# Block 0 of a two-layer transformer kernel: the fourth tile's transposition given to a DMA, and two Q chunks begun for three tiles

## The chip, the cores and the metric

The kernel runs on one core of a Trainium2 chip. The metric is the device time of one execution in microseconds (us), taken as the median of repeated runs.

## The reference

The input `x` has 2048 tokens of 1024 features in bf16. A layer normalisation, an attention and a residual sum are followed by a layer normalisation, a gated feed-forward part and a residual sum; the pair is done twice with the same weights.

```python
qkv = layernorm(x) @ wqkv                      # 32 heads of 32
idx = pos[:, None] - (arange(8) * 2)[None, :]  # 8 keys, every second token back
attn = softmax(q . k[idx] * 32**-0.5)          # negative positions masked
x = x + (attn @ v[idx]) @ wo
h = relu(layernorm(x) @ W_gate) * (layernorm(x) @ W_up)   # 3584 wide
x = x + h @ W_down
```

## The kernel before

The 2048 tokens are four blocks of 512, and a block is four tiles of 128 tokens. All of `x` stays in SBUF as sixteen tiles `x0` to `x15`. Matmuls need the normalised block with features on partitions, `xnT`, an array of tile, feature chunk (eight of 128) and token.

Only block 0 of the first layer is touched by the change. Its layer normalisation is `ln_first` and its V product is `v_first`; they are written out by hand, tile by tile, so that TensorE can start while most of the data is still in flight. The steps that matter:

- `bn` and `aggr` make mean and variance of a tile on VectorE, `power` makes the reciprocal deviation on GpSimd, and `apply(t)` writes the normalised tile into `xn_first` on VectorE.
- `turn(t)` transposes a tile with eight TensorE transposes into a PSUM tile (`tp_pair`); `copy(t, "v", 0)` and `copy(t, "a", 1)` bring the two halves into `xnT_first`, one on VectorE and one on ScalarE. `later(t)` is these three for tiles 2 and 3.
- Tile 0 is multiplied before its deviation is known. `scaled(i)` multiplies the deviation into its part of V; `widen` multiplies it into tile 0 of `xnT_first`, so that Q and K can use that tile as it is.
- `prod(kc, c, t0, t1)` is one V matmul: weight chunk `kc`, output chunk `c`, tiles `t0` to `t1`. Tiles 0 and 1 share the PSUM tiles `pairs[0, i]`, tiles 2 and 3 the PSUM tiles `pairs[1, i]`, one for each two output chunks. `halves(i, part, k0)` finishes one of these.

After V come sixteen groups `acc_q` and `acc_k` of eight matmuls with 512 columns (`qk_steps`), in the order q0, q1, q2, k0, q3, k1 and so on. ScalarE copies every finished PSUM tile to SBUF.

Weights are loaded in slabs of 1 MB into a ring of five buffers (`wring`): both halves of V (`v0, 0` for `kc` 0 to 3 and `v0, 1` for `kc` 4 to 7), both halves of Q, both of K. The sixth slab, the second half of K, takes the buffer of `v0, 0` and so can only be loaded when the last matmul that reads `v0, 0` is done. Nearly all DMAs are issued by SyncE (SP) in one written order (`sp_dma` ties each to the one before); in block 0 that order is the V slices with `x2` and `x3` among them, Q, `x4` and `x5`, the first K slab, the second K slab, `x6` to `x11`, and then the transposing DMAs of block 1 (`xnT_a`). ScalarE's queue issues only a part of `x0` and `x1`.

PSUM has six buffers for products, so a new product may have to wait until ScalarE or VectorE has read an old one. TensorE's order is fixed by `pe_group`, VectorE's by `dv`, ScalarE's in this part by `on("a", ...)`. Events with a planned time (`ev`) only set the order in which the program is written.

Of the kernel before, what the change touches and what calls it, by code (L numbers as in the profile page):

```python
# [8 lines left out]
F32 = mybir.dt.float32  # L9
# [4 lines left out]
P = 128  # L14
# [6 lines left out]
KC = D // P  # L21
BLK = 512
TPB = BLK // P
# [13 lines left out]
def kernel(  # L37
# [11 lines left out]
    nc = tc.nc  # L49
# [31 lines left out]
    psum = ctx.enter_context(tc.tile_pool(name="psum", bufs=6, space=bass.MemoryType.PSUM))  # L81
# [41 lines left out]
    @contextmanager  # L123
    def pe_group():
        if tail_pe[0] is None:
            yield
        else:
            with tc.issue_after(tail_pe[0]):
                yield

    def mm(*args, **kwargs):
        tail_pe[0] = nc.tensor.matmul(*args, **kwargs).ins  # L132
# [51 lines left out]
    slab = {}  # L184
# [9 lines left out]
    def qkv_half(i, hh):  # L194
        return wqkv_v[:, hh * (KC // 2):(hh + 1) * (KC // 2), i * D:(i + 1) * D]
# [26 lines left out]
    def load_slab(key, src):  # L222
        shp = list(src.shape)
        t = wring.tile([P, 8 * SLAB], BF16, tag="slab", name="w_" + "_".join(str(k) for k in key))
        tv = t[:, 0:shp[1] * shp[2]].rearrange("p (a b) -> p a b", b=shp[2])
        if key[0] == "v0":
            for i, (k0, k1) in enumerate(((0, 1), (1, 2), (2, 3), (3, 4)) if key[1] == 0 else ((0, 1), (1, 2), (2, 3), (3, 4))):
                if (key[1], i) == (1, 2):
                    load_x(0, [2, 3])
                sp_dma(tv[:, k0:k1, :], src[:, k0:k1, :])  # L230
        else:
            sp_dma(tv, src)
        slab[key] = tv
# [71 lines left out]
    load_slab(("v0", 0), qkv_half(2, 0))  # L305
    load_slab(("v0", 1), qkv_half(2, 1))
    load_slab(("qk01", "q", 0), qkv_half(0, 0))

    ones = const.tile([P, P], BF16, name="ones")
    nc.vector.memset(ones[:], 1.0)  # L310
# [9 lines left out]
    def ln_first():  # L320
# [94 lines left out]
        def open_up():  # L415
# [12 lines left out]
            apply(1, 0)  # L428
            apply(1, 1)

        hold.update(on=on, bn=bn, aggr=aggr, apply=apply, turn=turn, copy=copy, widen=widen,
                    spread_rstd=spread_rstd, open_up=open_up, last=last)
        return hold

# [3 lines left out]
    def v_steps(n, ln, key, early=False):  # L438
# [15 lines left out]

        return [f_(c) for c in range(KC)]

    def v_first(ln):
        st = att[0]
        pairs, opened = {}, set()

        def prod(kc, c, t0, t1):
            part = t0 // 2
            if (part, c // 2) not in pairs:
                pairs[part, c // 2] = psum.tile([P, 2, BLK // 2], F32, tag="acc", name="acc_v")
            acc = pairs[part, c // 2][:, c % 2, (t0 % 2) * P:(t0 % 2 + t1 - t0) * P]
            with pe_group():
                mm(acc, lhsT=slab["v0", kc // (KC // 2)][:, kc % (KC // 2), c * P:(c + 1) * P],
                   rhs=ln["xnT"][:, t0:t1, kc, :], start=(part, c // 2) not in opened, stop=(kc == KC - 1),
                   skip_group_check=True)
            opened.add((part, c // 2))  # L470

        def scaled(i):
            dv(nc.vector.tensor_tensor, st["vT"][:, 2 * i:2 * i + 2, 0:P], pairs[0, i][:, :, 0:P],
               _ap(ln["rb"], 0, [[0, 2], [1, P]]), op=ALU.mult)

        def later(t):
            ln["turn"](t)
            ln["copy"](t, "v", 0)
            ln["copy"](t, "a", 1)

        def halves(i, part, k0):
            for c in (2 * i, 2 * i + 1):
                for kc in range(k0, KC):
                    prod(kc, c, 2 * part, 2 * part + 2)

        def head():
            st["vT"] = big_tile([P, KC, BLK], "vT_0", True)
            ln["open_up"]()

            def chunk(kc, t):  # L490
                for c in range(KC):
                    prod(kc, c, t, t + 1)

            for kc in range(4):
                chunk(kc, 0)
            ln["turn"](1, (0,))
            ln["copy"](1, "v", 0)
            ln["turn"](1, (1,))
            ln["copy"](1, "a", 1)
            chunk(4, 0)  # L500
            for kc in range(5):
                chunk(kc, 1)
            ln["spread_rstd"]()
            chunk(5, 0)
            chunk(5, 1)
            ln["bn"](2, 0)
            ln["bn"](2, 1)
            ln["aggr"](2)
            ln["bn"](3, 0)
            ln["apply"](2)  # L510
            ln["bn"](3, 1)
            ln["aggr"](3)
            for i in range(KC // 2):
                if i == 2:
                    later(2)
                    scaled(1)
                    ln["apply"](3)
                halves(i, 0, 6)
                if i != 1:
                    scaled(i)  # L520
                ln["on"]("a", nc.scalar.copy, st["vT"][:, 2 * i:2 * i + 2, P:2 * P], pairs[0, i][:, :, P:2 * P])
            for t in (2, 3):
                for c in range(KC):
                    if (t, c) == (2, KC // 2):
                        later(3)
                        ln["widen"]()
                    for kc in range(KC // 2):
                        prod(kc, c, t, t + 1)
            for i in range(KC // 2):
                halves(i, 1, KC // 2)  # L530
                ln["on"]("a", nc.scalar.copy, st["vT"][:, 2 * i:2 * i + 2, 2 * P:BLK], pairs[1, i][:])
            tail_act[0] = ln["last"]["a"]

        return head
# [17 lines left out]
    def qk_steps(n, ln, key, staged=False):  # L552
        b = n % NB
        st = att[n]
        staging = {}

        def tile_of(nm, c, cols):
            if staged:
                staging[nm, c] = pool["stage"].tile([P, BLK], BF16, tag="st", name=f"{nm}st_{n}_{c}")
                return staging[nm, c][:]  # L560
            t = qk_pool.tile([P, cols], BF16, tag=nm, name=f"{nm}_{n}_{c}")
            st[(nm, c)] = t
            return t[:]

        def f_(nm, c):
            def f():
                if nm == "k" and c == 0 and not staged:
                    khalo[n] = qk_pool.tile([P, KC, HALO], BF16, tag="kh", name=f"kh_{n}", bufs=2)
                acc = psum.tile([P, BLK], F32, tag="acc", name=f"acc_{nm}")
                with pe_group():  # L570
                    for kc in range(KC):
                        w = slab[(key, nm, kc // (KC // 2))][:, kc % (KC // 2), bass.ds(c, P, KC)]
                        mm(acc[:], lhsT=w, rhs=ln["xnT"][:, :, kc, :], start=(kc == 0), stop=(kc == KC - 1))
                if nm == "q":
                    q = tile_of("q", c, BLK)
                    tail_act[0] = nc.scalar.copy(q, acc[:]).ins
                elif staged:
                    tail_act[0] = nc.scalar.copy(tile_of("k", c, BLK), acc[:]).ins
                else:
                    k = tile_of("k", c, HALO + BLK)  # L580
                    tail_act[0] = nc.scalar.copy(k[:, HALO:HALO + BLK], acc[:]).ins  # L581
                    if b == 0:
                        with (tc.issue_after(ln["last"]["g"]) if "last" in ln else nullcontext()):
                            nc.gpsimd.memset(k[:, 0:HALO], 0.0)
                    else:
                        nc.gpsimd.tensor_copy(k[:, 0:HALO], khalo[n - 1][:, c, :])
                    nc.gpsimd.tensor_copy(khalo[n][:, c, :], k[:, BLK:BLK + HALO])  # L587
            return f

        def put(nm, c):  # L590
            def f():
                sp_dma((q_d if nm == "q" else k_d)[c, :, b * BLK:(b + 1) * BLK], staging.pop((nm, c))[:])
            return f

        def get(nm, c):
            def f():
                lead = 0 if nm == "q" else HALO
                t = qk_pool.tile([P, lead + BLK], BF16, tag=nm, name=f"{nm}_{n}_{c}")
                st[(nm, c)] = t
                sp_dma(t[:], (q_d if nm == "q" else k_d)[c, :, b * BLK - lead:(b + 1) * BLK])  # L600
            return f

        order = QK_STAGED if staged else QK_ORDER
        steps = [f_(nm, c) for nm, c in order]
        if not staged:
            return steps
        return steps, [put(nm, c) for nm, c in order], [get(nm, c) for nm, c in order]
# [368 lines left out]
    head = v_first(ln_a[0])  # L976
    ev.append((0.25, head))
    ev.append((0.35, lambda: load_x(1, [0, 1])))
    ev.append((t_v0 + GRP * 6 + 0.5, lambda: load_x(1, [2, 3])))
    ev.append((t_v0 + GRP * 6 + 0.6, lambda: load_x(2)))  # L980
    ev.append((t_v0 + GRP * 6 + 0.7, zero_v))
    stats, apply, turn, ln_a[1] = ln_steps(1, "a", True, range(TPB))
# [154 lines left out]
```

## Time and profile before

| quantity | value |
|---|---|
| median of 3 runs | 1617.12 us (1616.38 to 1617.78) |
| profiled execution, its own time | 1616.67 us |
| its span, first to last instruction | 1615.0 us |
| TensorE (PE) busy | 1610.2 us |
| granted TensorE clock | 1.0 |
| DMA traffic | 317.94 MB, mean 197 GB/s |

The span is 1.67 us shorter than the execution's own time. The chain of waits follows the work that ended last back to the start; where it names only TensorE, a microsecond of TensorE is a microsecond of the kernel. Times inside the profile are counted from the span's start. "SPq" and "ACTq" are instructions that issue DMAs from SyncE and from ScalarE.

### The profile page before, as it was taken

The page shows a single profiled execution, that of the slowest core. Times are in us where ns is not written, and L with a number is a line of the kernel's source. Part 1 is how long each engine was busy: PE and PEld are TensorE (multiplying, and loading weights), DVE is VectorE, ACT ScalarE, POOL GpSimd, SP SyncE. Part 2 cuts the span into 40 slices and gives each one's busy share as a digit, 9 for nine tenths or more (in the row PEclk, how much of TensorE's full clock was granted, in tenths as well). Part 3 has the DMA queues.
Part 4 walks back from the last instruction along what each step waited for, and adds up shares of the span by engine and source line. Part 5 has one row for each costly group of instructions (what it writes and reads, how often), then busy time and mean ns, then how long its engine had stood idle before and what let it go on. Part 6 is the DMA issues. An engine that isn't in the chain of part 4 may idle for free.

```text
span 1615.0 us, 19088 instructions
## 1 busy us (share of the span) xinstructions
PE 1610.2 (100%) x7703; PEld 789.6 (49%) x7703; DVE 1141.2 (71%) x968; ACT 473.2 (29%) x967; POOL 177.6 (11%) x170
## 2 busy tenths in 40 slices
PE   9999999999999999999999999999999999999999
PEld 7646544444444445444454444544445444444445
DVE  6999989997989698929389293893939939311211
ACT  4753312132115313603136031361313311131110
POOL 2400000010003002300053000530005100000000
PEclk9999999999999999999999999999999999999999
DMA  9867867596668666784757857488574884655552
GB/s 308 182 193 244 215 178 239 183 225 199 205 199 220 199 185 204 198 247 146 224 159 204 234 158 228 153 205 249 166 225 157 204 243 157 209 158 180 157 167 68
DMA packets 359561, 317.94 MB, mean 197 GB/s; under 512 B 105136, under 2 KB 333616, under 8 KB 358960
## 3 DMA queue, kind: packets, MB, share of 16 engines
q1 hardware_dynamic: 358896, 316.13, 67.3%
q8 instruction: 60, 0.98, 0.3%
q10 hardware_dynamic: 576, 0.59, 0.1%
q14 instruction: 29, 0.24, 0.0%
HBM read 266.29 MB, written 34.66 MB: 186 GB/s over the span
## 4 chain that ended last, share of the span: by engine, by line
PE 99%; DMA 0%; DVE 0%; issue 0%; POOL 0%; ACTq 0%; DVEq 0%
PE acc_u L132 24%; PE acc_g L132 24%; PE dacc L132 18%; PE acc_k L132 7%; PE acc_wo L132 7%; PE acc_q L132 7%; PE acc_v L132 7%; PE dacc_pair L132 5%; DMA x<-in_A_x_dram 0%; DVE x L890 0%; DVE bst L106 0%; PE tp_pair L408 0%; POOL rstd L330 0%; PE L L132 0%; DVE xn_first L106 0%
## 5 line engine op out<-in xcount | busy, mean ns | idle before, releaser
L132 PE MATMUL acc_u<-xnT_b,w_u 128*128 128x512 bf16 x1792 | 423.3, 379 | 0.0
L132 PE MATMUL acc_g<-xnT_b,w_g 128*128 128x512 bf16 x1792 | 423.3, 379 | 0.0
L833 ACT ACTIVATE r<-acc_g 128x512 bf16<-128x512 f32 x224 | 133.6, 596 | 725.5 <-PE acc_g L132 676.2
L106 DVE TENSOR_TENSOR hT<-acc_u,r 128x512 bf16<-128x512 f32 x224 | 150.9, 687 | 240.8 <-PE acc_u L132 238.1
L132 PE MATMUL dacc<-w_d,hT 128*128 128x512 bf16 (+2 forms) x1456 | 305.0, 369 | 0.0
L132 PEld LDWEIGHTS <-hT 128*128 128x128 bf16 x1876 | 181.3, 98 | 206.0
L132 PEld LDWEIGHTS <-w_u 128*128 128x128 bf16 x1792 | 175.4, 98 | 211.4
L132 PEld LDWEIGHTS <-w_g 128*128 128x128 bf16 x1792 | 175.3, 98 | 211.4
L106 DVE TENSOR_TENSOR pv<-a,vhm 128x4096 bf16<-128x4096 bf16 x64 | 143.5, 2284 | 0.0
L890 DVE TENSOR_TENSOR x<-dacc,x 128x512 bf16<-128x512 f32 (+2 forms) x40 | 24.9, 653 | 154.2 <-PE dacc L132 154.2
L646 DVE TENSOR_TENSOR t<-q,k 128x2048 f32<-128x2048 bf16 x56 | 128.0, 2292 | 6.7 <-ACT k L581 4.6
L106 DVE TENSOR_TENSOR t<-q,k 128x2048 f32<-128x2048 bf16 x56 | 127.5, 2287 | 3.3 <-ACT k L581 1.8
L106 DVE TENSOR_TENSOR pv<-pv 128x1024 bf16<-128x1024 bf16 (+1 forms) x128 | 113.8, 951 | 0.0
L132 PE MATMUL acc_wo<-w_o,oT 128*128 128x512 bf16 x512 | 111.8, 379 | 0.0
L662 DVE TENSOR_TENSOR ac<-ac,t 128x2048 f32<-128x2048 f32 x48 | 109.7, 2285 | 0.3
L106 DVE TENSOR_TENSOR ac<-ac,t 128x2048 f32<-128x2048 f32 x48 | 109.7, 2285 | 0.0
L587 POOL COPY kh<-k 128x14 bf16<-128x14 bf16 x40 | 52.1, 1306 | 502.1 <-ACT k L581 502.1
L265 POOL TENSOR_TENSOR st_b<-st_b,neg_half 128x1 f32<-128x1 f32 x29 | 43.6, 1510 | 528.8 <-ACT st_b L264 528.8
L132 PE MATMUL dacc_pair<-w_d,hT 128*128 128x512 bf16 (+1 forms) x420 | 92.9, 372 | 0.0
L132 PEld LDWEIGHTS <-oT 128*128 128x128 bf16 x512 | 50.1, 98 | 60.3
L260 ACT ACTIVATE xn_b<-x 128x1024 bf16<-128x1024 bf16 x29 | 30.3, 1045 | 131.7 <-DVE x L106 69.5
L452 ACT CAST vT<-acc_v 128x512 bf16<-128x512 f32 x56 | 32.5, 587 | 56.7 <-PE acc_v L132 55.7
(144 smaller groups left out, 1231.2 us busy)
## 6 DMA issues: line engine op xcount, KB each, us to landing
w_g<-in_B_W_gate_dram SPq DMA_DIRECT2D x56, 1024.0 KB, 7.3
w_u<-in_B_W_up_dram SPq DMA_DIRECT2D x56, 1024.0 KB, 5.5
w_d<-in_B_W_down_dram SPq DMA_DIRECT2D x48, 1024.0 KB, 6.3
w_o<-in_A_wo_dram SPq DMA_DIRECT2D x16, 1024.0 KB, 8.5
vhm<-v_d SPq DMA_DIRECT2D x32, 284.0 KB, 6.8
v_d<-vT SPq DMA_DIRECT2D x8, 1024.0 KB, 9.9
oT<-o_d SPq DMA_DIRECT2D x32, 256.0 KB, 3.9
w_d<-in_B_W_down_dram SPq DMA_DIRECT2D x16, 512.0 KB, 3.7
```

The source lines that it names most:

```text
L106: tail_dve[0] = f(*args, **kwargs).ins
L132: tail_pe[0] = nc.tensor.matmul(*args, **kwargs).ins
L260: nc.scalar.activation(xn, xt[:], ACT.Square, accum_out=sq)
L265: nc.gpsimd.tensor_tensor(rstd, vpe, neg_half[:, 0:1], op=ALU.pow)
L452: tail_act[0] = nc.scalar.copy(st["vT"][:, c, :], acc[:]).ins
L587: nc.gpsimd.tensor_copy(khalo[n][:, c, :], k[:, BLK:BLK + HALO])
L646: nc.vector.tensor_tensor(t[:], i0, i1, op=ALU.mult)
L662: nc.vector.tensor_tensor(o, i0, i1, op=ALU.add)
L833: tail_act[0] = nc.scalar.activation(rs[j][:], acc[:], ACT.Relu).ins
L890: run = dv if n < NB - 2 else (lambda f, *args, **kwargs: f(*args, **kwargs))
```

## The change

Five things are changed, all in the first 30 us.

1. Tile 3 is no longer transposed on TensorE. `turn_by_dma(3)` issues one transposing DMA from ScalarE's queue, straight from `xn_first` to `xnT_first`; the two copies from PSUM go with it. `apply(3)` moves ahead of it, and both of tile 3's `bn` move ahead of `apply(2)`.
2. V of tile 2 is now multiplied over all eight weight chunks at once, with 128 columns; V of tile 3 comes later and also with 128 columns, where the second half of the weight chunks used to be done for both tiles with 256 columns.
3. Between them stand the first two Q chunks for tiles 0 to 2 (`early_q`, 384 columns). After V of tile 3, `qk_steps` adds the last 128 columns to them. `widen` comes ahead of V of tile 2.
4. The second Q slab is loaded by an explicit call and the last two slices of the V slab are one DMA.
5. `x6` and `x7` are issued ahead of the second K slab instead of behind it.

```diff
-            for i, (k0, k1) in enumerate(((0, 1), (1, 2), (2, 3), (3, 4)) if key[1] == 0 else ((0, 1), (1, 2), (2, 3), (3, 4))):
+            for i, (k0, k1) in enumerate(((0, 1), (1, 2), (2, 3), (3, 4)) if key[1] == 0 else ((0, 1), (1, 2), (2, 4))):
...
     load_slab(("qk01", "q", 0), qkv_half(0, 0))
+    load_slab(("qk01", "q", 1), qkv_half(0, 1))
...
+        def turn_by_dma(t):
+            on("a", nc.scalar.dma_start_transpose, hold["xnT"][:, t, :, :], xna[:, t, :])
...
-        def later(t):
-            ln["turn"](t)
-            ln["copy"](t, "v", 0)
-            ln["copy"](t, "a", 1)
-
-        def halves(i, part, k0):
+        def halves(i):
             for c in (2 * i, 2 * i + 1):
-                for kc in range(k0, KC):
-                    prod(kc, c, 2 * part, 2 * part + 2)
+                for kc in range(6, KC):
+                    prod(kc, c, 0, 2)
+
+        def early_q(c):
+            acc = psum.tile([P, BLK], F32, tag="acc", name="acc_q")
+            st[("acc_q", c)] = acc
+            with pe_group():
+                for kc in range(KC):
+                    mm(acc[:, 0:3 * P], lhsT=qk_weight("qk01", "q", kc, c), rhs=ln["xnT"][:, 0:3, kc, :],
+                       start=(kc == 0), stop=(kc == KC - 1), skip_group_check=True)
...
             ln["bn"](3, 0)
-            ln["apply"](2)
             ln["bn"](3, 1)
             ln["aggr"](3)
+            ln["apply"](2)
             for i in range(KC // 2):
                 if i == 2:
-                    later(2)
+                    ln["turn"](2)
+                    ln["copy"](2, "v", 0)
+                    ln["copy"](2, "a", 1)
+                    ln["apply"](3)
+                    ln["turn_by_dma"](3)
                     scaled(1)
-                    ln["apply"](3)
-                halves(i, 0, 6)
+                halves(i)
...
-            for t in (2, 3):
-                for c in range(KC):
-                    if (t, c) == (2, KC // 2):
-                        later(3)
-                        ln["widen"]()
-                    for kc in range(KC // 2):
-                        prod(kc, c, t, t + 1)
+            ln["widen"]()
+            for c in range(KC):
+                for kc in range(KC):
+                    prod(kc, c, 2, 3)
+            for c in range(2):
+                early_q(c)
+            for c in range(KC):
+                for kc in range(KC // 2):
+                    prod(kc, c, 3, 4)
             for i in range(KC // 2):
-                halves(i, 1, KC // 2)
+                for c in (2 * i, 2 * i + 1):
+                    for kc in range(KC // 2, KC):
+                        prod(kc, c, 3, 4)
...
-                acc = psum.tile([P, BLK], F32, tag="acc", name=f"acc_{nm}")
+                acc = st.pop((f"acc_{nm}", c), None)
+                t0 = 0 if acc is None else TPB - 1
+                if acc is None:
+                    acc = psum.tile([P, BLK], F32, tag="acc", name=f"acc_{nm}")
                 with pe_group():
                     for kc in range(KC):
-                        w = slab[(key, nm, kc // (KC // 2))][:, kc % (KC // 2), bass.ds(c, P, KC)]
-                        mm(acc[:], lhsT=w, rhs=ln["xnT"][:, :, kc, :], start=(kc == 0), stop=(kc == KC - 1))
+                        mm(acc[:, t0 * P:BLK], lhsT=qk_weight(key, nm, kc, c), rhs=ln["xnT"][:, t0:TPB, kc, :],
+                           start=(kc == 0 and t0 == 0), stop=(kc == KC - 1), skip_group_check=(t0 > 0))
...
-    ev.append((t_v0 + GRP * 6 + 0.5, lambda: load_x(1, [2, 3])))
+    ev.append((t_v0 + GRP * 6 + 0.2, lambda: load_x(1, [2, 3])))
```

More of the change, by code (lines that the diff above doesn't have):

```diff
@@ L429, in open_up @@
             apply(1, 1)
-        hold.update(on=on, bn=bn, aggr=aggr, apply=apply, turn=turn, copy=copy, widen=widen,
+        def turn_by_dma(t):
+            on("a", nc.scalar.dma_start_transpose, hold["xnT"][:, t, :, :], xna[:, t, :])
+        hold.update(turn_by_dma=turn_by_dma, on=on, bn=bn, aggr=aggr, apply=apply, turn=turn, copy=copy, widen=widen,
                     spread_rstd=spread_rstd, open_up=open_up, last=last)
@@ L455, in v_steps, with qk_weight @@
         return [f_(c) for c in range(KC)]
+    def qk_weight(key, nm, kc, c):
+        return slab[(key, nm, kc // (KC // 2))][:, kc % (KC // 2), bass.ds(c, P, KC)]
     def v_first(ln):
```

## The prediction

> **What bounds the kernel now.** I read first the chain that ended last on the profile's page: it is TensorE throughout.
>
> ```profile
> PE 99%; DMA 0%; DVE 0%; issue 0%; POOL 0%; ACTq 0%; DVEq 0%
> ```
>
> Then the same chain in order of time around the change (start, length, what). From 9.16 us on no wait stands in it, so whatever TensorE saves or loses here comes out at the end.
>
> ```profile
> 12.12 1.77 PE acc_v L132 x24
> 13.88 0.45 PE tp_pair L408 x8
> 14.33 1.77 PE acc_v L132 x24
> 16.10 0.45 PE tp_pair L408 x8
> 16.54 6.17 PE acc_v L132 x80
> 22.72 5.18 PE acc_q L132 x24
> 27.90 1.73 PE acc_k L132 x8
> ```
>
> The second `tp_pair` row, 0.45 us, is what the change takes off TensorE. Third, the timeline where tile 3 is prepared: what the new DMA must wait for.
>
> ```profile
> 14.37 0.42 DVE L106 COPY xnT_first<-tp_pair 128x512 bf16<-128x512 bf16 x1 [0.39 <-PE tp_pair L408]
> 14.82 0.59 ACT L330 COPY xnT_first<-tp_pair 128x512 bf16<-128x512 bf16 x1 [0.17 <-DVE xnT_first L106]
> 15.04 0.54 DVE L106 TENSOR_SCALAR xn_first<-x,mv,rstd 128x1024 bf16<-128x1024 bf16 x1
> ```
>
> Fourth, SyncE's queue in the timeline (start, time in issue, count), and the busy times by stretch, whose last columns are clock, DMA share and GB/s.
>
> ```profile
> 9.59 10.04 SPq L121 DMA_DIRECT2D w_qk_k<-in_A_wqkv_dram  x2
> 19.68 3.96 SPq L121 DMA_DIRECT2D x<-in_A_x_dram  x6
> 25.22 5.11 SPq L121 DMA_TRANSPOSE xnT_a<-xn_a  x2
> ```
>
> ```profile
> 16.00:20.00 4.00, 4.00 (x67) 3.91 (x65) 3.08 (x5) 1.24 (x3) 0.00 (x0) 1.00 1.05 386
> 20.00:22.00 2.00, 2.00 (x20) 1.80 (x19) 1.86 (x8) 1.29 (x3) 0.55 (x1) 1.00 0.84 179
> ```
>
> The second K slab spans the pause from 9.59: SyncE stood until TensorE freed its buffer and issued it at 19.3. All 16 DMA engines are full from 16 to 20 us, exactly when tile 3 now has to pass through them.
>
> **TensorE's own work.** Row prices: 48 matmuls of 128 columns in 2.68 us are 55.8 ns each; the 6.17 us row holds 48 of those and 32 of 256 columns, so 109 ns each; eight of 512 columns in 1.73 us are 216 ns each. Removed: eight transposes, -0.45. V of tiles 2 and 3 was 64 x 55.8 + 32 x 109 ns = 7.06 us and becomes 128 x 55.8 ns = 7.14, +0.08. The two Q chunks were 16 x 216 ns; they become sixteen of 384 and sixteen of 128 columns. No row has 384 columns: between the price of 256 (109) and of 512 (216) the ends are 0.9 us less and 0.9 us more; I take the middle, 163, as the two rows lie on a line through nearly zero, so +0.04. Sum: -0.33 us.
>
> **TensorE's new times, if nothing waits.** The first eight transposes end at 14.33, the eight matmuls of 256 columns at 15.20, tile 2 (64 x 55.8 ns) at 18.77, the early Q (16 x 163 ns) at 21.38; V of tile 3 then takes 1.79 for each half of the weight chunks, to 23.17 and 24.96; the rest of Q chunks 0 and 1 ends at 25.85, q2 at 27.58, and k0 reaches its fifth matmul, the first to read the second K slab, at 28.44.
>
> What these steps need: tile 2's ScalarE half, used now at 15.42 instead of after tile 3, is copied by 15.41: allow 0.05. `widen` (1.22) now follows three `scaled` (0.4 each) from 15.3 and ends near 17.8, under tile 2 until 18.77; without that cover it would cost its overrun. The Q slabs were issued at 6.9 and 7.56 and landed 7.4 and 10.5 later, at 14.3 and 18.1; needed at 18.77 and 19.4. Merging two V slices only spares SyncE one issue of 0.43 us; those bytes keep their place and their matmuls came without a wait: nothing. Moving both `bn` ahead of `apply(2)` delays it by 0.6 us to about 13.1, under matmuls until 13.88: nothing.
>
> **The DMA's price on ScalarE.** The copy ends at 15.41 and `apply(3)` near 15.3, so it is issued at about 15.45. Single-tile transposing issues from SyncE held that queue for 1.25 to 3.77 us, the long ones with much queued before them. Behind it on ScalarE stand the V copies for pairs 2 and 3 (0.35 each), and their PSUM buffers are what the two early Q chunks wait for at 18.77 and 20.1. With 1.3 us the copies are done at 17.1 and 17.4: hidden. With 3.77 the first is late by 0.8. ScalarE's queue is empty, so I take 1.3.
>
> **Its landing.** With a nearly idle queue (issue at 324.11) the first packet starts 1.2 us later, 1024 packets of 256 bytes run in 1.5 us at 18 ns each, and it lands 3.2 us after issue. That would be 18.65 here, long before 21.4: the lower end, no wait. But SyncE's backlog at that moment is `x5`, the first K slab and now `x6` and `x7` too: 896 packets of 2048 bytes, 56 for each DMA engine; `x5` and that slab, 40 for each, took 3.7 us, 92 ns a packet. How two queues share an engine shows in the packet records of the first 5 us, when `x1` came over ScalarE's queue: in the middle of its transfer 114 packets of it stand beside 131 of SyncE's, turn about. With turns of one packet, tile 3's 64 packets for each engine finish with the backlog: from 16.65, 56 x 92 + 64 x 18 ns is 6.3 us, to 23.0; with the 0.5 us that the idle row took from its last packet to landing, 23.5. Loads in this full stretch landed up to 2.0 us after their last packet, which makes 25.0 the upper end. I take 23.5, because the sharing row is of this very pair of queues and the idle row is not. TensorE wants it at 21.4: +2.1.
>
> [...]
>
> **The second K slab.** Its buffer is free after the first half of tile 3's V: 19.2 before, 23.17 in the new times. From there to its first use were 9.5 us and are now 5.27 (1.79 + 0.89 + 1.73 + 0.86). It was issued 0.1 us after release and landed 5.9 us after issue, with the queue run nearly dry: 6.0, late by 0.7. Other 1 MB loads landed in 4.9 to 6.0 us, so 0 to 0.8; I take 0.7, from the same load. `x6` and `x7` are ahead of it but gone by about 23.0. Behind its wait on SyncE stand `x8` to `x11` (ScalarE first reads `x8` at 33.6; they land near 31) and block 1's transposes (first read at 50): nothing. If tile 3 waits, release and use move together and the 0.7 stays.
>
> **Sum.** -0.33 + 0.05 + 2.1 + 0.7 = +2.5 us. The profiled execution took 1616.67 (span 1615.0 and 1.67 around it), the runs' median is 1617.12. That gives 1619.2 or 1619.6; I say 1619.4, which counts from 1616.9. After 30 us the queues keep their order but for a few ScalarE copies near 85 us, under a chain with no wait. A change of less than 0.2%, 3.2 us, is what a measurement of this kernel can't tell from none.
>
> **The rivals.**
> - *Forecast, 41%*: turn about, landing at 22.5 to 24.2 with the slab's 0.7; +1.5 to +3.2, so 1618.4 to 1620.1. Within 0.2%.
> [...]
> - *Slower by over 0.2%, 27%*: the sixteen engines don't reach a transposing row together, or the landing lags as in the full stretch. From a landing at 24.2 it decides; at 25.0, wait 3.6, the sum is +4.0, and with a slow issue on ScalarE or a K slab at 6.5 us some +5: 1620.1 to 1621.9. For it: 256-byte packets that took up to 0.9 us each in the burst at 28 us. Against it: the DMA work in sight ends at 23.0.
> - *Faster by over 0.2%, 3%*: nothing in the profile gives more than the transposes' 0.45 us; this is for what I don't see downstream.
>
> So faster 0.03, same 0.41 + 0.29 = 0.70, slower 0.27. The range takes in the hidden case and most of the slow one, leaving out its upper end and the 3%: 1616.6 to 1621.6.
>
> **What would show it.** Right: no second `tp_pair` row in the chain; a DMA_TRANSPOSE on ACTq near 15.45, about 1.3 us long, landing 8 us after issue; V of tile 3 held some 2.1 us after the last 384-column matmul, then 0.7 us before k0's fifth matmul. Wrong: the transpose landing under 6 us, TensorE waiting for a V copy on ScalarE at 18.77, a K slab landing in under 5.2 us, or a wait in the chain after 32 us.

## The result, and the profile after

| | median | runs | profiled execution | its span |
|---|---|---|---|---|
| before | 1616.4 us | 1616.3 to 1617.78 | 1616.67 us | 1615.0 us |
| after | 1622.93 us | 1621.93 to 1623.1 | 1622.93 us | 1621.2 us |

After is 1.0038 times before, with an interval of 1.0027 to 1.0049: slower by about 6 us, where +2.5 had been forecast and the range ended at 1621.6. The side was that of the rival *slower by over 0.2%*, but even its price, +4.0 to +5, was too small.

The chain that ended last, on the page of after, now has one part in a hundred that is not TensorE:

```profile
PE 99%; DMA 1%; DVE 0%; issue 0%; DVEq 0%
```

The same chain in order of time (start, length, what) shows where that one part is:

```profile
13.48 0.46 PE tp_pair L409 x8
...
14.31 0.54 DVE xn_first L106
14.84 0.03 DVE vT L106
14.88 11.12 DMA xnT_first<-xn_first
26.00 0.04 issue
26.04 5.36 PE acc_v L132 x64
31.40 2.72 PE acc_q L132 x24
34.12 1.73 PE acc_k L132 x8
```

There is one `tp_pair` row instead of two, as meant. In its place the chain runs from `apply(3)` through the transposing DMA, 11.12 us long, into V of tile 3. The timeline has the issue and the stop, in brackets behind the row of V:

```profile
14.88 1.34 ACTq L331 DMA_TRANSPOSE xnT_first<-xn_first  x1
...
18.41 2.77 PE L132 MATMUL acc_q<-xnT_first,w_qk_q 128*128 128x384 bf16 x16
...
26.04 5.36 PE L132 MATMUL acc_v<-xnT_first,w_v 128*128 128x128 bf16 x64 [4.87 <-DMA xnT_first<-xn_first]
```

TensorE had done everything that stands ahead of tile 3's V in its order at 21.17 and stood until 26.04. The stretches of the profile add the second half of the story (columns: stretch, its length, busy time of PE, PEld, DVE, ACT and POOL with counts, granted TensorE clock, DMA share, GB/s):

```profile
18.00:21.00 3.00, 3.00 (x27) 2.67 (x25) 1.83 (x5) 0.00 (x0) 0.10 (x1) 1.00 1.07 382
21.00:26.00 5.00, 0.18 (x2) 0.00 (x0) 2.84 (x7) 0.00 (x0) 1.23 (x2) 1.00 0.72 110
26.00:28.00 2.00, 1.96 (x24) 1.96 (x24) 1.93 (x6) 0.00 (x0) 0.78 (x1) 0.65 0.00 0
28.00:30.00 2.00, 2.00 (x22) 2.00 (x20) 1.49 (x5) 0.00 (x0) 0.84 (x2) 0.50 0.00 0
30.00:32.00 2.00, 2.00 (x37) 2.00 (x36) 0.23 (x1) 1.97 (x5) 0.00 (x0) 1.00 0.80 197
```

After the stop the granted clock is 0.5, from 26.6 to 30.0, and only 24 and 22 matmuls are done in two stretches of 2 us; when it is 1.00 again, 37 are. The 64 matmuls took 5.36 us where 64 of 55.8 ns would be 3.57.

So the account, between two points that both kernels pass, the end of tile 2's eight transposes and the start of k0: before 27.90 - 14.33 = 13.57 us, after 34.12 - 13.94 = 20.18, which is +6.61. Of it 4.87 is the stop, 1.79 the clock, and -0.05 is left for everything else. The spans differ by 6.2, because after came to the first point 0.39 earlier. In after and the kernels made from it, whose edits all come later, the row of 48 V matmuls begins anywhere from 8.76 to 9.33 and once, in e8, at 11.15, so a difference of 0.39 is within the head's own scatter.

### The profile page after: what moved, and what is told of

It reads as the page before. It is cut to its first block, busy times and chain, and to the rows that moved or that the text cites. A ratio compares the mean times of both kernels' runs of the same rounds, so it can differ in the third digit from the quotient of the medians.

```text
span 1621.2 us, 19166 instructions
## 1 busy us (share of the span) xinstructions
PE 1612.2 (99%) x7743; PEld 792.8 (49%) x7743; DVE 1140.4 (70%) x967; ACT 471.9 (29%) x966; POOL 178.4 (11%) x170
## 4 chain that ended last, share of the span: by engine, by line
PE 99%; DMA 1%; DVE 0%; issue 0%; DVEq 0%
PE acc_u L132 24%; PE acc_g L132 24%; PE dacc L132 18%; PE acc_wo L132 7%; PE acc_k L132 7%; PE acc_v L132 7%; PE acc_q L132 7%; PE dacc_pair L132 5%; DMA xnT_first<-xn_first 1%; PE scratch L132 0%; DVE x L910 0%; PE tp L409 0%; PE tp_pair L409 0%; PE L L132 0%; DVE xn_first L106 0%
## 5 line engine op out<-in xcount | busy, mean ns | idle before, releaser
L607 POOL COPY kh<-k 128x14 bf16<-128x14 bf16 x40 | 56.0, 1405 | 507.1 <-ACT k L601 507.1
```

## The experiments

**The theories.** *Shared engines* (mine after the result): the transpose lands late because its packets go through the same sixteen DMA engines as what SyncE has already queued, and the stop it causes costs more than itself, because the clock falls afterwards. *Rival 1*: a transpose from ScalarE's queue takes such a time whatever else is queued. *Rival 2*: the loss is in the new order of the matmuls. *Rival 3*: V of tile 3 is slow by itself in its new place, with or without a stop. Every kernel below is compared with before run on the same chip, 1616.67 or 1616.68 us in the median.

**e1: the turn back on TensorE, the new order kept.**

```diff
-                    ln["turn_by_dma"](3)
...
+            ln["turn"](3)
+            ln["copy"](3, "v", 0)
+            ln["copy"](3, "a", 1)
             for c in range(2):
                 early_q(c)
```

> The changed kernel with tile 3 turned on TensorE again (eight transposes ahead of the early Q, and the two copies), all else as changed. Theory 1 (the transposing DMA and the pause it makes are the whole loss): no wait in TensorE's chain, the 0.45 us of transposes come back, so 1616.5 (1615.8 to 1617.5), level with before. Rival 2 (the new order itself costs: narrow matmuls, buffers, the late second K slab): the loss stays, at least 1618.5. If the second K slab is late by itself, a wait of up to 0.8 us stands before the fifth matmul of k0.

Measured: 1617.48 us (1617.19 to 1617.73), 1.0005 times before (0.9995 to 1.0014). In its chain the stop is gone:

```profile
18.74 0.45 PE tp_pair L409 x8
19.19 2.61 PE acc_q L132 x16
21.79 1.80 PE acc_v L132 x32
23.59 0.02 issue
23.61 5.48 DMA w_qk_k<-in_A_wqkv_dram
```

TensorE goes from the eight transposes into the early Q and V without a pause. The loss sits in the DMA turn, and rival 2 falls as its cause. A little of it stays, less than the times can tell from none: from the end of tile 2's transposes to the end of k0 e1 took 16.12 us where before took 15.29. The last row is the second K slab, of which the waits leave 0.2 us (0.4 when counted by the starts of k0's matmuls):

```profile
PE acc_k L132 <- DMA w_qk_k<-in_A_wqkv_dram: 0.2, 1, 0.2
```

**e2: less in SyncE's queue beside the transpose.** The first K slab is issued from ScalarE behind the transpose, and `x6` and `x7` go back behind the second K slab.

```diff
+                    load_slab(("qk01", "k", 0), qkv_half(1, 0), lambda d, s: ln["on"]("a", nc.scalar.dma_start, d, s))
...
-    ev.append((t_v0 + GRP * 6 + 0.2, lambda: load_x(1, [2, 3])))
+    ev.append((t_v0 + GRP * 6 + 0.5, lambda: load_x(1, [2, 3])))
```

> The DMA still turns tile 3 from ScalarE's queue, but the first K slab is issued on ScalarE's queue behind it, and x6 and x7 behind the second K slab, so SyncE's queue holds only the end of Q, x4 and x5 when the transpose is issued at 14.9. Theory 1 (it shares the DMA engines with SyncE's backlog): it lands by 20 us, no wait on it in the chain, TensorE's clock stays at 1.0, 1616.3 (1615.6 to 1617.4). Rival 1 (a transpose from ScalarE's queue takes some 11 us whatever else is queued): it lands at 25 or later and the time stays above 1621.5.

Measured: 1617.74 us (1617.53 to 1619.89), 1.0008 (0.9998 to 1.0017). The DMA issues (last number: median us from issue to landing):

```profile
xnT_first<-xn_first ACTq DMA_TRANSPOSE x1, 5.0
```

The same DMA from the same queue lands after 5.0 us instead of 11.1, at 20.5, ahead of its use; the granted clock stays 1.00, and V of tile 3 takes 3.57 us. Rival 1 falls: what else is queued decides. The time is 0.3 above the range expected; the profile has a wait of 0.6 us in the attention (see e6) and k0 0.2 us longer than before's.

**e3: matmuls in the stop.** 22 matmuls that compute nothing used stand between the early Q and V of tile 3.

```diff
             for c in range(2):
                 early_q(c)
+            scratch(22)
```

> The changed kernel with 22 idle matmuls of 512 columns (4.75 us) on TensorE between the early Q and V of tile 3; they compute nothing that is used. The transpose still lands near 26. Theory 1, clock part (the granted clock of 0.5 to 0.65 from 26 to 30 us comes from TensorE standing still): the clock stays at 1.0 and V of tile 3 takes 3.6 us instead of 5.4, so 1.8 us less than the changed kernel, 1621.1 (1620.4 to 1621.8). Rival 3 (V of tile 3 is slow for another reason, as SBUF traffic or narrow matmuls): V of tile 3 stays at 5.4 and the time at 1622.9.

Measured: 1622.5 us (1621.57 to 1623.15), 1.0036 (1.0023 to 1.0049). The chain of e3, and a stretch of it (columns as above):

```profile
21.69 4.75 PE scratch L132 x22
26.44 3.57 PE acc_v L132 x64
```

```profile
26.00:30.00 4.00, 4.00 (x70) 3.82 (x68) 2.01 (x6) 1.29 (x3) 0.84 (x2) 1.00 0.10 14
```

Without a stop the clock stays 1.00 and the 64 matmuls take 3.57 us. From the end of tile 2's transposes to the start of k0 e3 took 18.30 us, 1.88 less than after, as expected. The total shows only 0.4 of that, and missed the range: e3's head came 0.50 later and k0 took 0.18 longer, and the profiled execution spent 2.5 us outside its span where after's spent 1.7. Why it did is open; in no other kernel here is it over 1.8. The DMA landed 9.9 us after issue, at 25.3, and the filler ran on to 26.44, 1.1 us past it, so a shorter one could save more (e7).

**e5: the turn issued by SyncE**, in its one queue, behind what is already there and ahead of the rest.

```diff
-            on("a", nc.scalar.dma_start_transpose, hold["xnT"][:, t, :, :], xna[:, t, :])
+            sp_dma(hold["xnT"][:, t, :, :], xna[:, t, :], True)
```

> The same transposing DMA issued on SyncE's queue instead of ScalarE's, behind the Q slabs and ahead of x4, x5 and the first K slab, which wait for its issue. Theory 1: nothing shares the engines with it but the end of Q, it lands 3 to 4.5 us after issue, by 20 us; no wait in the chain; 1616.4 (1615.6 to 1617.4). If a transposing DMA is slow in this stretch on any queue (rival 1b, say by SBUF traffic of the other engines), it lands after 22 and the time is above 1618.

Measured: 1617.38 us (1617.07 to 1619.25), 1.0006 (0.9997 to 1.0016). Its DMA issues and its timeline:

```profile
xnT_first<-xn_first SPq DMA_TRANSPOSE x1, 3.6
```

```profile
15.39 1.35 SPq L121 DMA_TRANSPOSE xnT_first<-xn_first  x1
```

It holds SyncE for 1.35 us, lands at 19.0 and nothing waits for it. SyncE issues its loads in a written order, so the transpose comes ahead of those that after lets run beside it, with only the end of Q before it.

**e6: only `x6` and `x7` back behind the second K slab.**

```diff
-    ev.append((t_v0 + GRP * 6 + 0.2, lambda: load_x(1, [2, 3])))
+    ev.append((t_v0 + GRP * 6 + 0.5, lambda: load_x(1, [2, 3])))
```

> The changed kernel with x6 and x7 issued behind the second K slab again (part 5 undone): SyncE's backlog beside the transpose is 256 packets of 2048 bytes shorter and ends with the first K slab near 20.3. Theory 1 (the transpose ends when the backlog does): landing at 22 to 23.5 instead of 26, a wait of 0.5 to 2 us, no fall of the clock, 1617.3 to 1619.0. Rival 1 (its own slowness): landing at 25 or later, time at 1622 or more.

Measured: 1619.37 us (1619.22 to 1622.82), 1.0019 (1.0009 to 1.0028). Its chain and its waits (total, times, longest):

```profile
15.22 7.68 DMA xnT_first<-xn_first
...
22.94 1.96 PE acc_v L132 x32
```

```profile
PE acc_v L132 <- DMA xnT_first<-xn_first: 1.4, 1, 1.4
```

Half a megabyte less beside it brings the landing from 11.1 us after issue (9.9 and 9.8 in e3 and e7, which have the same queue as after) to 7.7 and the stop from 4.9 to 1.4; the clock stays 1.00. One matmul of the attention also waits 0.6 us for VectorE (`L` for `s`), as it does in e2 and e10, which have the two tiles back too, but not in e9 or before; what of the order brings it was not followed up. The time is 0.4 above the range expected. Its +2.7 lies beside the forecast's +2.5 by luck: the forecast counted `x6` and `x7` in the queue beside the transpose, and its steps were others.

**e7: a filler that ends ahead of the landing**, eight matmuls that compute nothing used.

```diff
+            scratch(8)
```

> The changed kernel with 8 idle matmuls (1.7 us) between the early Q and V of tile 3, so that TensorE stands still for 2 to 3 us instead of 4.9 ahead of V of tile 3; landing as before at 25 to 26. If the clock falls only after a longer stop than that, it stays at 1.0, V of tile 3 takes 3.6 us, and the time is 1.8 us under the changed kernel's, 1620.2 to 1621.3. If any stop of over a microsecond lets it fall, V of tile 3 stays near 5.4 and the time at 1622.5 to 1623.

Measured: 1620.95 us (1620.57 to 1621.4), 1.0027 (1.0017 to 1.0037). Chain and stretches:

```profile
15.33 9.81 DMA xnT_first<-xn_first
25.14 0.04 issue
25.19 3.73 PE acc_v L132 x64
```

```profile
24.00:26.00 2.00, 0.81 (x15) 0.81 (x15) 1.93 (x5) 0.00 (x0) 0.25 (x1) 1.00 0.02 6
26.00:28.00 2.00, 2.00 (x40) 2.00 (x38) 1.93 (x6) 0.38 (x1) 0.70 (x2) 1.00 0.00 0
```

The DMA is still late, but TensorE stands for 1.8 us only, and the clock is 1.00 right after: 40 matmuls in 2 us where after had 22. The 64 matmuls take 3.73 us, not 5.36, and the kernel is 2.0 us under after although it does eight matmuls more. Not all of that is the clock: up to the start of k0 e7 is 2.94 us under after, 1.63 from the 64 matmuls and 1.31 because the DMA landed sooner, and a later head gives part of it back. Rival 3 falls, and the clock's price is 1.63 us here, 1.79 in e3.

**e4: the DMA turn alone, in the old order of the matmuls.** Before, with one edit:

```diff
-                        later(3)
+                        on("a", nc.scalar.dma_start_transpose, ln["xnT"][:, 3, :, :], ln["xna"][:, 3, :])
```

> The kernel before with one thing changed: tile 3 turned by the DMA on ScalarE's queue instead of by TensorE, in the old order without the early Q. It is issued near 16.6 beside a backlog that ends at 20.3 and wanted at 17.9. Theory 1: landing at 21.5 to 23, wait 3.6 to 5 us, and if the stop is long enough a slower clock after it: 1619.5 to 1622.5. Rival 1 (11 us whatever is queued): landing at 27.5, at least 1625. Rival 4 (the new order is what makes the DMA late): no loss, 1616.5.

Measured: 1624.68 us (1623.67 to 1625.55), 1.0049 (1.0036 to 1.0063), above the range expected of shared engines and just under the 1625 of rival 1, whose landing at 27.5 it does not have. Chain and a stretch:

```profile
16.22 6.88 DMA xnT_first<-xn_first
23.10 0.04 issue
23.14 7.64 PE acc_v L132 x64
```

```profile
24.00:26.00 2.00, 2.00 (x22) 2.00 (x20) 0.00 (x0) 0.00 (x0) 0.00 (x0) 0.50 0.00 0
```

The DMA lands in 6.9 us, a little faster than e6's, but its use comes earlier here: a stop of 6.4 us, half clock from 20.94, inside the stop, to 27.76, and the 64 matmuls (32 narrow, 32 of 256 columns) take 7.64 us instead of 32 x 55.8 + 32 x 109 ns = 5.28. That makes 6.4 + 2.36 - 0.45 = +8.3, near the +8.0 between the medians. The new order is not what makes the DMA late, and it does something: the early Q covers the stop in part, and without it a DMA that landed sooner costs more.

**e8, e9, e10: is there a version that gains?** All three issue the turn from SyncE as in e5. e8 keeps only the first early Q chunk; e9 has none and puts `x6` and `x7` back; e10 keeps both and puts `x6` and `x7` back.

```diff
-            for c in range(2):
-                early_q(c)
+            early_q(0)
```

> The transpose on SyncE's queue ahead of x4, x5 and the first K slab, and only the first Q chunk begun early, so that V of tile 3 starts 1.3 us sooner and the second K slab's buffer is free sooner. Theory 1: landing by 19.2, wanted at 20.4, no wait in the chain, TensorE's own work 0.35 us under before: 1616.1 to 1617.0, which the times can't tell from before; the chain must show it. If SyncE's later issue of x4 to x7 and the first K slab costs, a wait stands at k0 or in VectorE's work of block 1.

> The transpose on SyncE's queue ahead of x4, x5 and the first K slab, x6 and x7 behind the second K slab, and no early Q: V of tile 3 follows V of tile 2 at once. TensorE's own work is 0.45 us of transposes less and 0.08 of narrower matmuls more than before. If the transpose lands 3.1 to 3.6 us after issue at 15.4, by 19.0, it is wanted at 19.1 and the second K slab's buffer is free at 20.9: no wait, 1616.1 to 1616.8, which the times can't tell from before's 1616.7; the chain shows it. If it lands later, or the K slab does, each microsecond late is a microsecond: 1617 to 1618.

> The same with the two Q chunks begun early, as in the change: the transpose has 2.6 us of cover, but the second K slab's buffer is free 2.6 us later, at 23.5, with its first use 5.3 us after that. Landing of the slab 5.4 to 6 us after issue: a wait of 0.2 to 0.8 us ahead of the fifth matmul of k0, 1616.9 to 1617.8, not under e9.

Measured: e8 1617.68 us, 1.0006 (0.9997 to 1.0015); e9 1616.88, 1.0003 (0.9994 to 1.0012); e10 1617.78, 1.0007 (0.9998 to 1.0016). None can be told from before; e8 and e9 lie 0.7 and 0.1 above the ranges expected. The profile of e8 is of its slowest execution, whose second K slab held k0 back by 0.6 us. The chain of e9:

```profile
13.74 0.45 PE tp_pair L409 x8
...
15.32 7.18 PE acc_v L132 x124
22.50 5.19 PE acc_q L132 x24
27.69 1.73 PE acc_k L132 x8
```

There is no long stop in this part, tile 3's transposes are off TensorE, and yet the way from the end of tile 2's transposes to the end of k0 is 15.23 us where before has 15.29. The 124 narrow matmuls take 7.18 us where 124 of 55.8 ns would be 6.92. They have not become slower: within tile 2 and within tile 3 they start 55.8 ns apart. Two short pauses make the difference, 0.20 us ahead of tile 2's fifth matmul, which is the first to read the half that ScalarE copies, and 0.10 us ahead of tile 3, whose DMA landed at 18.7 (3.6 us after its issue at 15.13). With 0.08 for the narrower matmuls, of the 0.45 hardly anything is left.

The first pause is in every kernel with the new order. In after's timeline ScalarE's copy ends at 15.00, and TensorE goes on at 15.06:

```profile
14.42 0.58 ACT L331 COPY xnT_first<-tp_pair 128x512 bf16<-128x512 bf16 x1 [0.17 <-DVE xnT_first L106]
...
15.06 3.33 PEld L132 LDWEIGHTS <-w_v 128*128 128x128 bf16 x59 [0.15 <-issue]
```

## Why the prediction was wrong, step by step

The terms of the sum, forecast and then measured in after: the wait for tile 3 +2.1 and 4.87, the second K slab +0.7 and nothing, TensorE's own work -0.33 and about -0.22, ScalarE's half of tile 2 +0.05 and 0.20, and the clock, which had no term, 1.79. The wait and the clock are what failed.

**Right.** The issue held ScalarE for 1.34 us (1.3 foreseen), and the V copies behind it came in time for the early Q. `widen`, the merged V slices and the moved `bn` cost nothing that shows. The two queues did share the engines evenly, by count: in the packet records of after from 19.0 to 21.5 us, 423 transposing packets of 256 bytes stand beside 406 load packets of 2048 bytes. How an engine chooses between the queues the records don't show. A transpose that stays hidden beside SyncE's full queue, the case of the 0.29 among the chances, no run shows: there it landed 6.9 (e4) to 11.1 us (after) after its issue, and without a filler it came ahead of its use only with less in that queue (e2, 5.0) or from that queue itself (e5, 3.6).

**Wrong: from issue to first packet.** I took 1.2 us from the row of a nearly idle queue, so a start at 16.65. It was 4.1 us, at 18.99. The runs show what it depends on. From ScalarE's queue beside SyncE's full one it was 4.1 in after, e3, e6 and e7 and 3.6 in e4; in e2, where SyncE had only the end of Q, `x4` and `x5` queued, 1.9; in SyncE's own queue, behind the end of Q (e5, e8, e9, e10), 1.3. I had let the transpose take turns from its first microsecond. What holds the first packet back is not shown, only that it came later with more queued. That alone moves 23.0 by 2.9, less what the backlog had shrunk meanwhile.

**Wrong: all sixteen engines at work to the end.** At 22.0 to 23.0 almost nothing moves in after: 10 packets of the two queues begin in that microsecond, and 17 packets of both stand for 1.4 to 1.6 us each, from 21.8 to 23.5. The last transposing packet ends at 25.46 and the DMA lands at 26.0. The upper end of my landing was 25.0, and the rival *slower by over 0.2%* named this trouble as a guess. How much of the lateness is the standstill's is not shown: e3, with the same queue and only one long packet, landed 9.9 us after issue all the same, at 25.3. In e6 and e4, which have `x6` and `x7` behind the second K slab, there is no such standstill, and there the landing was 22.9 and 23.1. That is near the 23.5 taken, but with a later start and a smaller backlog than were counted.

**Missing: the clock.** The sum priced a wait at its own length. The stop of 4.87 us cost 1.79 more, because most of tile 3's V ran at half the rate: 22 matmuls in the 2 us from 28.0, where e7 has 40 in the 2 us from 26.0. Of the 6.61 us, this is the term that appears nowhere in the prediction, not even in the slow rival. In after the granted clock fell to 0.5 at 26.60, 0.55 us after TensorE had started again, and was 1.00 again at 30.01, 3.41 us later. In e4 it fell at 20.94, 4.2 us into the stop, and was half for 6.83 us. What sets these moments is not shown. In e4 TensorE had been idle for all of the 3.41 us before the fall, but in after these held 0.56 us of matmuls, and in e8 they held 1.93 (stretches as above):

```profile
4.36:7.78 3.42, 1.93 (x21) 1.07 (x20) 2.80 (x7) 2.20 (x6) 0.30 (x2) 1.00 1.02 347
7.78:11.19 3.41, 3.41 (x35) 3.41 (x34) 1.16 (x4) 0.44 (x2) 1.59 (x4) 0.50 1.03 394
```

There the clock was half in the head of the profiled execution, and its row of 48 began 2 us late, though TensorE's longest pauses before were 0.78 and 0.58 us. Stops of 1.4 and 1.8 us (e6, e7) left the clock alone where 4.87 and 6.4 us (after, e4) did not, but the length of a stop alone does not decide it.

**Mis-sized: the second K slab.** The mechanism is right, and the 0.7 is not. Without a stop it was 0.2 to 0.4 (e1: 5.5 us from issue) and 0.6 in e8, whose slab took 7.1. In after it was nothing: issued at 29.17, landed 5.3 us later at 34.5 and wanted at 35.0, since the half clock delayed its use too. I had let release and use move together.

**Mis-sized: TensorE's own work, and the 0.05.** Not -0.33 but about -0.22: the sixteen early matmuls took 2.61 us, as priced, when V followed at once (e1), and the finish of Q with q2 took 2.72 where 2.62 was counted. The wait for ScalarE's half of tile 2, for which 0.05 was allowed, is the 0.20 shown at e9. Together they eat most of what eight transposes gave.

## What to carry to other kernels

Before you hand a transposition to a DMA, list what is already queued for the same engines at that moment: here the issuing queue's being empty was worth nothing, and the same 256 KB took 3.6 us on SyncE's queue ahead of the loads and 11.1 us on the empty queue beside them. Price a stop of TensorE with the clock it can lose: at 4.9 us it cost 1.8 more, and eight idle matmuls that shortened the stop to 1.8 (e7) kept the clock at 1.00. And count the gain to the last tenth first: with 0.45 us of transposes to win, 0.08 given back by narrower matmuls and 0.30 by two short pauses, even the version without a long wait could not be told from before.

## What the runs showed of the hardware that I had not expected

- The granted clock after a stop: 1.00 after 1.4 and 1.8 us, half after 4.87 and 6.4 us. No run lies between, and in e8 it was half from 7.78 to 11.19 us after pauses of 0.78 and 0.58 us, so where it turns is not shown.
- The first packet of a transposing DMA came 1.3 us after its issue on SyncE's queue behind the end of Q, and 3.6 to 4.1 us on an idle second queue beside a full one.
- A standstill with transposing packets in flight, and its cause stays open. In after it follows a packet of 16384 bytes on the queue that loads instructions, which took 1.09 us at 21.51; in e7 14 packets stood from 22.5 to 23.9 after such a packet of 1.30 us at 21.76; in e6 such a packet came at 22.30, as the last transposing packets ended, and in e4 at 26.07, and neither has a standstill of this size. But in e3 the packet took 1.64 us at 21.95 and only one other packet was long, and in e2 23 packets stood from 17.7 to 19.4 with no such packet near. Moving that instruction load by itself was not tried.
